# Weights through casting DMAs, q and k in longer runs, and a new order of loads, in a fused attention and SwiGLU kernel

## The chip, the cores and the metric

One core of one Trainium2 chip. The metric is device time in microseconds (us) of one execution. All executions in this study counted as fast (none stood apart by its time or its granted clock), so all numbers may be compared. The engines are PE (matmul), PEld (its weight load), DVE (VectorE), ACT (ScalarE), POOL (GpSimd) and SP (issues DMAs).

## The reference

Attention over q, k, v of shape (4, 8, 768, 64): a query sees its last 96 keys and the first 8 keys of its sequence ("global" keys), with a linear bias by distance. Then RMS norm and a SwiGLU feed-forward of 3072 tokens (512 to 1536 to 512). Inputs and output are fp32; both kernels multiply in bf16.

```python
scores = scale * np.matmul(q, k.transpose(0, 1, 3, 2))
keep = is_global | is_local                     # key < 8, or 0 <= query - key < 96
dist = np.where(is_global & ~is_local, 96., np.abs(rel))
a = softmax(np.where(keep, scores - slopes * dist, -1e9))
x = (a @ v).transpose(0, 2, 1, 3).reshape(3072, 512)
xn = x / np.sqrt(np.mean(x * x, -1) + 1e-6) * rms_g
g, val = xn @ w_gate, xn @ w_val
return (g * sigmoid(g) * val) @ w_out
```

## The kernel before

The tokens go through in 8 chunks of 384 (three blocks of 128; chunk c is half c % 2 of batch c // 2). A chunk has four head pairs. For a pair: POOL casts q and k to bf16 (`cast`), PE transposes them (`tr`), DVE copies the transposes out of PSUM into `qT` and `kT` (`cp`), PE makes two groups of scores (`qk`: d=0 against the query's own block, d=1 against the block before, whose first eight keys are overwritten with the global keys), ACT takes exponentials (`ex`), DVE masks, PE multiplies by v (`av`) and DVE normalises (`norm`). Then come the RMS norm (`ssq`, `rstd`, `xn`), a transpose (`xtr`) and its eviction by ACT (`xev`). The feed-forward has 12 F units a chunk (w_gate and w_val matmuls, tanh, two DVE multiplications) and O units (w_out).

The order is fixed by hand in slots: one unit per slot, with a `pre` list before its matmuls and a `post` list after. The program order that results is the order of each engine's queue, and also what decides which of two accesses of a buffer comes first.

Weights come in fp32 through a staging pool and are cast by three engines:

```python
def load_w(what, s):
    if what == "o":
        t = wstg.tile([128, 4, 512], F32, tag="ws", name="wso")
        nc.sync.dma_start(t, moe_w_out[ds(512 * s, 512)].rearrange("(f p) c -> p f c", p=128))
    ...
def cast_w(what, s):
    t = wst.pop((what, s))
    if what == "g":
        nc.vector.tensor_copy(w_gate[:, :, ds(512 * s, 512)], t)
    elif what == "v":
        nc.gpsimd.tensor_scalar(w_val[:, :, ds(512 * s, 512)], t, 0.5, None, op0=ALU.mult)
    else:
        nc.scalar.copy(w_out[:, ds(4 * s, 4), :], t)
```

q, k and v come per head pair, a token of a block per partition (runs of 256 bytes); the loads of chunk 0 are shared by SP and ACT. The copy of transposes and the global keys:

```python
def cp(c, p):                                   # DVE
    ...
    nc.vector.tensor_copy(qT, t[:, 0])
    nc.vector.tensor_copy(kT[:, ds(CH * half, CH)], t[:, 1])

def ex(c, p, d):                                # ACT
    ...
    if d == 0:                                  # global keys into the first 8 columns of each block
        nc.gpsimd.tensor_copy(
            kT.rearrange("p (j t) -> p j t", t=128)[:, lo:hi, 0:NG], _brd(kT[:, 0:NG], 1, hi - lo))

def attention(c, starts, gap, early=False):
    for p, a in enumerate(starts):
        at_slot(pre, a - 1, cast, c, p)
        at_slot(post, a, tr, c, p)
        at_slot(pre, a + 1, cp, c, p)
        at_slot(post, a + 1, qk, c, p, 0, early)
        at_slot(pre, a + 2, ex, c, p, 0)
        at_slot(pre, a + 3, mask, c, p, 0)
        at_slot(post, a + 1 + gap, qk, c, p, 1, early)
        ...
        at_slot(post, a + 3 + gap, av, c, p)
        at_slot(pre, a + 4 + gap, norm, c, p)
    ...
attention(0, [1, 3, 5, 7], 1, early=True)       # then F units of chunk 0, with attention 1 among them
```

The softmax here doesn't subtract the row's maximum and nothing guards it: scores larger than these inputs give would overflow.

## Time and profile before

| | before |
|---|---|
| median of 4 runs | 325.44 us (324.91 to 325.94) |
| span of the profiled run | 324.4 us, mean granted clock 0.967 |
| first scores / first gate matmul of chunk 0 / of chunk 1 | 17.4 / 45.5 / 92.0 us |
| two steady chunks | 65.0 us |

The gate matmuls are the `gps` group, the first of a chunk's feed-forward. Of chunk 1's, two ran at 92.0 us and the rest from 93.7; the prediction cuts at 93.7. The period of two steady chunks is the distance between the first gate matmuls of chunks two apart.

The prediction shows the stages and the timelines. Three more lines will be needed for comparison. The first two are PE's waits from 93.7 us to the end (who waited, for whom: us in all, times, longest); the third is from POOL's timeline of set-up (start, length).

```profile
PE trp L226 <- ACT xT L349: 5.7, 5, 1.1
PE avp L303 <- DVE P L288: 4.0, 12, 0.6
```

### The profile page before, as it was taken

The numbers are of one execution on the slowest core, as the hardware profiler recorded it, in microseconds if no ns is written. First come the engines' busy times: TensorE is split into PE (matmuls) and PEld (weight loads), VectorE is DVE, ScalarE is ACT, GpSimd is POOL, SyncE is SP. The second block draws the span as 40 slices with busy tenths as digits, with TensorE's granted clock in tenths as the row PEclk, the third lists the DMA queues.
The fourth block names the chain that finished last, engine by engine and source line by source line (L and its number), as shares of the span: only waits on it lengthen the run. The fifth ranks groups of instructions, "written<-read, shape, count | busy, mean of one in ns | idle before, by whom it ended". The sixth has DMA issues, their size and how long they took to land.

```text
span 324.4 us, 5608 instructions
## 1 busy us (share of the span) xinstructions
PE 258.3 (80%) x2033; PEld 147.0 (45%) x2048; DVE 210.1 (65%) x463; ACT 159.5 (49%) x334; POOL 110.4 (34%) x225
## 2 busy tenths in 40 slices
PE   1055065849379999899989998999899989999995
PEld 0033033525135555455446654654466546544652
DVE  7265747696717576389748963897489738962860
ACT  0445133524377365755465557564655575646331
POOL 6470879650325550101365501013655010001000
PEclk9999999786959999999999999999999999999999
DMA  9993096619992171897019007970100020002002
GB/s 174 264 261 129 0 246 190 230 33 315 218 217 59 61 155 32 181 239 116 2 65 179 3 2 179 239 117 2 66 32 3 2 81 16 2 2 97 0 3 97
DMA packets 83835, 34.96 MB, mean 108 GB/s; under 512 B 76128, under 2 KB 76128, under 8 KB 83808
## 3 DMA queue, kind: packets, MB, share of 16 engines
q1 hardware_dynamic: 79008, 33.43, 45.6%
q10 hardware_dynamic: 4800, 1.18, 2.1%
q8 instruction: 16, 0.26, 0.4%
q14 instruction: 11, 0.09, 0.1%
HBM read 28.31 MB, written 6.29 MB: 107 GB/s over the span
## 4 chain that ended last, share of the span: by engine, by line
PE 42%; DVE 30%; ACT 16%; issue 6%; DMA 2%; POOL 1%; ACTq 1%; DVEq 0%; POOLq 0%
PE ops L378 12%; PE gps L361 10%; PE vps L367 9%; DVE hb L371 7%; DVE u L370 7%; PE sc L255 4%; ACT P L266 4%; DVE xn L333 4%; ACT xT L349 4%; ACT t L364 3%; DVE P L285 3%; DVE P L288 3%; DVE w_gate L121 2%; ACT junk L319 2%; PE avp L303 2%
## 5 line engine op out<-in xcount | busy, mean ns | idle before, releaser
L266 ACT ACTIVATE P<-sc,bias 128x384 bf16<-128x384 f32 (+1 forms) x128 | 63.7, 551 | 49.7 <-PE sc L255 49.7
L361 PE MATMUL gps<-xT,w_gate 128*128 128x384 bf16 x384 | 83.8, 341 | 1.3 <-ACT xT L349 1.2
L367 PE MATMUL vps<-xT,w_val 128*128 128x384 bf16 x384 | 82.3, 339 | 0.0
L370 DVE SCALAR_TENSOR_TENSOR u<-t,gps 128x384 f32<-128x384 f32 x96 | 53.0, 552 | 28.8 <-ACT t L364 26.9
L364 ACT ACTIVATE t<-gps 128x384 f32<-128x384 f32 x96 | 47.2, 491 | 48.5 <-PE gps L361 48.3
L378 PE MATMUL ops<-w_out,hb 128*128 128x512 bf16 x273 | 66.6, 380 | 0.6
L371 DVE TENSOR_TENSOR hb<-u,vps 128x384 bf16<-128x384 f32 x96 | 53.2, 554 | 10.4 <-PE vps L367 0.8
L367 PEld LDWEIGHTS <-w_val 128*128 128x128 bf16 x384 | 39.0, 102 | 28.3 <-issue 5.3
L361 PEld LDWEIGHTS <-w_gate 128*128 128x128 bf16 x384 | 34.5, 101 | 24.5 <-issue 5.1
L274 POOL COPY kT<-kT 128x16 bf16<-128x16 bf16 x32 | 6.3, 197 | 112.1 <-PE sc L255 101.6
L255 PE MATMUL sc<-qT,kT 64*128 64x128 bf16 x352 | 22.9, 233 | 21.1 <-DVE kT L237 18.6
L378 PEld LDWEIGHTS <-hb 128*128 128x128 bf16 x288 | 26.4, 98 | 28.2
L333 DVE TENSOR_SCALAR xn<-xu,r 128x512 bf16<-128x512 bf16 x24 | 17.0, 762 | 17.7 <-POOL r L326 17.7
L349 ACT ACTIVATE xT<-xtp,rmsg 128x384 bf16<-128x384 bf16 x32 | 16.8, 578 | 22.2 <-PE xtp L341 22.2
L255 PEld LDWEIGHTS <-kT 64*128 64x128 bf16 x352 | 10.9, 97 | 35.1 <-DVE kT L237 21.2
L319 ACT ACTIVATE junk<-xu 128x512 bf16<-128x512 bf16 x24 | 14.8, 619 | 20.9 <-DVE xu L312 20.8
L341 PE MATMUL xtp<-ident,xn 128*128 128x128 bf16 x96 | 10.6, 240 | 18.1 <-DVE xn L333 15.5
L288 DVE TENSOR_TENSOR P<-P,md 128x512 bf16<-128x512 bf16 (+1 forms) x32 | 15.7, 490 | 13.1 <-ACT P L266 13.1
L324 POOL TENSOR_SCALAR m<-ssq 128x3 f32<-128x3 f32 x8 | 1.6, 197 | 65.0 <-ACT junk L319 65.0
L226 PE MATMUL trp<-ident,qb 128*128 128x128 bf16 x96 | 11.7, 237 | 11.6 <-ACT xT L349 6.8
L209 POOL CAST V<-sv 128x384 bf16<-128x384 f32 (+1 forms) x40 | 20.3, 532 | 1.0 <-DMA sv<-in_v_dram 1.0
L236 DVE COPY qT<-trp 128x384 bf16<-128x384 bf16 x32 | 11.5, 359 | 13.8 <-PE trp L226 13.8
(54 smaller groups left out, 287.9 us busy)
## 6 DMA issues: line engine op xcount, KB each, us to landing
out_dram<-osb SPq DMA_DIRECT2D x24, 256.0 KB, 2.0
sq<-in_q_dram SPq DMA_DIRECT2D x12, 384.0 KB, 5.7
sk<-in_k_dram SPq DMA_DIRECT2D x12, 384.0 KB, 6.3
sv<-in_v_dram SPq DMA_DIRECT2D x12, 384.0 KB, 6.4
wsg<-in_moe_w_gate_dram SPq DMA_DIRECT2D x3, 1024.0 KB, 5.4
wsv<-in_moe_w_val_dram SPq DMA_DIRECT2D x3, 1024.0 KB, 5.5
wso<-in_moe_w_out_dram SPq DMA_DIRECT2D x3, 1024.0 KB, 6.9
sq<-in_q_dram SPq DMA_DIRECT2D x16, 96.0 KB, 3.6
```

The lines of the kernel that those rows point to most:

```text
L255: nc.tensor.matmul(sc[hh][:, ts(i, 128)], kT[r, ts(J, 128)], qT[r, ts(i, 128)], start=True, stop=True)
L266: nc.scalar.activation(P[:, hh, lo:HB, :], sc[hh][:, ds(128 * lo, CH - 128 * lo)], AF.Exp, bias=(bias1 if d else bias0)[:, h:h + 1], scale ...
L288: nc.vector.tensor_tensor(P[:, :, lo:HB, :], P[:, :, lo:HB, :], _brd(md1[:, ds(2 * p, 2)], 2, HB - lo), op=ALU.mult)
L319: nc.scalar.activation(junk, xus[c][:, i].rearrange("p h d -> p (h d)"), AF.Square, accum_out=at["ssq", c][:, i:i + 1])
L333: nc.vector.tensor_scalar(t[:, i], xus[c][:, i].rearrange("p h d -> p (h d)"), r[:, i:i + 1], None, op0=ALU.mult)
L349: nc.scalar.activation(xTs[c][:, 2 * j + cc, :], t[:, cc], AF.Copy, scale=rmsg[:, 2 * j + cc:2 * j + cc + 1])
L361: nc.tensor.matmul(g[:, 0:CH], w_gate[:, cc, ts(f, 128)], xTs[c][:, cc, :], start=(cc == 0), stop=(cc == CC - 1))
L364: nc.scalar.activation(t, g[:, 0:CH], AF.Tanh, scale=0.5)
L367: nc.tensor.matmul(vv[:, 0:CH], w_val[:, cc, ts(f, 128)], xTs[c][:, cc, :], start=(cc == 0), stop=(cc == CC - 1))
L370: nc.vector.scalar_tensor_tensor(u, t, 1.0, g[:, 0:CH], op0=ALU.add, op1=ALU.mult)
L371: nc.vector.tensor_tensor(hb[c][:, f, :], u, vv[:, 0:CH], op=ALU.mult)
L378: nc.tensor.matmul(o, hb[c][:, f, ts(j, 128)], w_out[:, f, :], start=(f == 0), stop=(f == FC - 1))
```

## The change

The intent: no engine spends time on casting weights, ACT is free of DMA issues at the start, q and k come in fewer and longer pieces, and loads are asked for in the order in which they are needed.

```diff
     def load_w(what, s):                      # POOL issues; the DMA casts on its way
         if what == "o":
-            t = wstg.tile([128, 4, 512], F32, tag="ws", name="wso")
-            nc.sync.dma_start(t, moe_w_out[ds(512 * s, 512)].rearrange("(f p) c -> p f c", p=128))
+            nc.gpsimd.dma_start(w_out[:, ds(4 * s, 4), :],
+                                moe_w_out[ds(512 * s, 512)].rearrange("(f p) c -> p f c", p=128))
 ...                                           # cast_w is gone; its 0.5 moves to the output eviction
+            nc.sync.dma_start(                 # three neighbouring tokens per partition, 768 bytes
+                st[name, c][:, ds(h0, n)],
+                src[b, ds(h0, n), ds(CH * half, CH)].rearrange("h (p i) d -> p h (i d)", i=HB))
 ...                                           # v: one block, all heads, per DMA
+    nc.vector.tensor_tensor(gl1, _brd(slope[0:NG], 2, 128), _brd(iidx, 1, H), op=ALU.mult)
 ...                                           # set-up: two such in place of five small ones per head
+            if c == 0 and name == "q":
+                nc.scalar.copy(o, i)           # chunk 0: q cast by ACT, k by DVE
+            elif c == 0:
+                nc.vector.tensor_copy(o, i)
 ...
+    def glob_v(c):                             # global rows of v: a DMA issued by POOL
 ...
-        nc.vector.tensor_copy(qT, t[:, 0])
-        nc.vector.tensor_copy(kT[:, ds(CH * half, CH)], t[:, 1])
+        nc.vector.tensor_copy(qT.rearrange("p (t i) -> p t i", i=HB),
+                              t[:, 0].rearrange("p (i t) -> p t i", i=HB))
+        nc.vector.tensor_copy(kT[:, ds(CH * half, CH)].rearrange("p (t i) -> p t i", i=HB),
+                              t[:, 1].rearrange("p (i t) -> p t i", i=HB))
 ...
+        late = 2 if early else 0               # norm of chunk 0 two slots later
-            at_slot(pre, a + 4 + gap, norm, c, p)
+            at_slot(pre, a + 4 + gap + late, norm, c, p)
 ...                                           # xtr and xev two slots later after xn
-    n0 = attention(0, [1, 3, 5, 7], 1, early=True)
+    cast_v(0, i) for the blocks; glob_v(0)     # (written shorter here)
+    for s in range(2):
+        load_w("g", s)
+        load_w("v", s)
+    stage(1)
+    nc.gpsimd.memset(st["q", 1][0:1, 0, 0:1], 0.0)   # holds chunk 1's loads back till here
+    load_qk(1, 0, 4); load_qk(1, 4, 4); load_v(1, i) for the blocks
+    load_w("g", 2)
+    load_w("v", 2)
+    for s in range(3):
+        load_w("o", s)
+    n0 = attention(0, [1, 3, 5, 7], 0, early=True)
-    units += [None] * 4
+    units += [None] * 11
-    e1 = attention(1, [s0 - 1, s0 + 1, s0 + 3, s0 + 5], 2)
+    e1 = attention(1, [s0 + 5, s0 + 7, s0 + 9, s0 + 11], 1)
-        e = attention(c, [f - 23, f - 19, f - 15, f - 11], 2)
+        e = attention(c, [f - 25, f - 21, f - 17, f - 13], 2)
```

Since a partition now holds tokens 3t, 3t+1, 3t+2, the transposes come out interleaved, and the two DVE copies put them back in order by reading PSUM with a step.

## The prediction

> **What bounds it now.** I first cut the span into stages, at the moments when the matmuls of a stage begin, and asked for the busy time of each engine in each stage. Columns: start:end in us, length, then busy us and (instructions) of each engine, granted clock, DMA share, GB/s.
>
> ```profile
> 0.00:17.40 17.40, 0.98 (x8) 0.51 (x10) 9.41 (x54) 3.28 (x3) 8.88 (x30) 1.00 1.08 230
> 17.40:31.40 14.00, 8.53 (x98) 5.58 (x98) 8.82 (x22) 7.29 (x16) 6.97 (x20) 1.00 0.80 194
> 31.40:45.50 14.10, 2.59 (x19) 1.90 (x20) 7.77 (x5) 4.05 (x10) 11.81 (x16) 1.00 0.32 93
> 45.50:93.70 48.20, 31.30 (x227) 17.47 (x226) 31.74 (x53) 19.34 (x39) 24.48 (x36) 0.84 0.87 200
> 93.70:321.40 227.70, 214.94 (x1687) 121.56 (x1701) 152.39 (x330) 125.47 (x267) 58.27 (x124) 0.99 0.35 75
> ```
>
> The reader is to see three regions. Up to 17.4 us PE does almost nothing (set-up). From 17.4 to 93.7 us (attention of chunk 0, its normalisation, feed-forward of chunk 0 with attention of chunk 1) PE is busy 42.4 of 76.3 us. From 93.7 us on, PE is busy 94%: seven chunks at 227.7/7 = 32.5 us each. A change that touches no matmul can win only a little there, and up to some tens of us in the first 93.7.
>
> Then the timelines of single engines (start, length, engine, line, what; in brackets idle time and its releaser) for the waits of the first part:
>
> ```profile
> 10.36 1.28 ACT L168 ACT_TABLE_LOAD   x1 [10.36 <-DMA sv<-in_v_dram]
> 13.69 1.21 DVE L175 TENSOR_TENSOR gl<-gl,inv 8x1024 f32<-8x1024 f32 x1 [5.84 <-ACT gl L169]
> 17.37 0.34 PEld L255 LDWEIGHTS <-kT 64*128 64x128 bf16 x8 [11.89 <-DVE kT L237]
> ...
> 34.61 5.38 POOL L123 TENSOR_SCALAR w_val<-wsv 128x2048 bf16<-128x2048 f32 x1
> 34.66 6.49 DVE L333 TENSOR_SCALAR xn<-xu,r 128x512 bf16<-128x512 bf16 x3 [3.25 <-POOL r L326]
> ...
> 91.24 1.90 ACT L125 CAST w_out<-wso 128x2048 bf16<-128x2048 f32 x1
> 93.02 1.06 ACT L349 ACTIVATE xT<-xtp,rmsg 128x384 bf16<-128x384 bf16 x2
> ```
>
> ACT issues loads of k and v, and those waits sit in front of its table load and mask exponentials; DVE waits for them, and the first scores wait for DVE. Later the xn scaling takes 6.49 us beside a POOL weight cast, where in steady state three of them take 0.88 (at 130.84 us, POOL idle) to 2.4 us. Just before the feed-forward of chunk 1, an ACT weight cast of 1.9 us stands ahead of the last xT eviction.
>
> By line and form, the casts that the change removes:
>
> ```profile
> L123 POOL TENSOR_SCALAR w_val<-wsv 128x2048 bf16<-128x2048 f32 x3 | 16.1, 5369 | 0.0
> L121 DVE CAST w_gate<-wsg 128x2048 bf16<-128x2048 f32 x3 | 8.8, 2948 | 0.0
> L125 ACT CAST w_out<-wso 128x2048 bf16<-128x2048 f32 x3 | 5.7, 1892 | 0.0
> L236 DVE COPY qT<-trp 128x384 bf16<-128x384 bf16 x32 | 11.5, 359 | 13.8 <-PE trp L226 13.8
> L237 DVE COPY kT<-trp 128x384 bf16<-128x384 bf16 x32 | 11.1, 347 | 0.0
> ```
>
> The last two rows are not removed but become strided.
>
> **The Trainium skill.** "SBUF — State Buffer", section "Who interferes with whom": DVE copies, casts and tensor_scalar in two-port modes and any GpSimd instruction exclude each other for the whole instruction. The trace agrees: the same w_gate cast takes 1.36 us with no POOL weight cast beside it, 3.48 and 4.00 beside one. "DMA: Bandwidth & Descriptors", section "SWDGE vs HWDGE vs iDMA": a cast during DMA needs the software path, whose descriptors GpSimd cores write; its section "Anatomy of one DMA" puts about 2 us fixed on such a DMA, mostly completion, and calls generation "small, variable". The trace of before has no such DMA, so nothing there tells how long POOL is held. "VectorE: DVE Perf Modes", section "What auto-detection actually checks": the doubled 16-bit mode needs steps of one. The trace fits: bf16 copies from PSUM take 0.35 us for 384 elements, f32 work on 384 takes 0.55 (hb row, 554 ns).
>
> **The change, part by part.**
>
> (1) Set-up. ACT loses its 12 DMA issues, so the exponentials start when gl1 and gl0 exist. Twice 1.2 us on DVE (the form of L175) after iota gives about 4.3; the mask copy 0.4; ACT twice 1.05, to 6.8; DVE 1.2 + 1.2 for the m products, to 9.2; memsets, k cast, transposes, two copies: first scores near 12 instead of 17.4 us. Loads of 768-byte runs instead of 256 should not hold this up: 2.36 MB at the 230 GB/s of this stage is 10 us, and the first pair is there near 4.
>
> (2) A new gate on POOL. As built, POOL's order for chunk 0 is: three v casts, two VG copies, one software DMA for the global rows, four weight DMAs, a memset, five weight DMAs, and only then the four kT copies on which each pair's second score group (d=1) waits. Before, the first kT copy was at 17.97 us. The last two weight DMAs also wait for the global-row DMA and the first weight slice to land. My estimate: v casts and VG copies finish near 11 (loads in order, each 0.2 to 0.26 MB, about 1 us), the global-row DMA near 12, nine weight DMAs at about 1.1 us of POOL each (an estimate; no row of before measures it) gives 22, the landing of slice 0 near 17 not being last. So d=1 of pair 0 goes at 22 instead of 18.2, although its first scores could be 5 us earlier.
>
> (3) Attention of chunk 0. Before, first scores at 17.4 to the last avp at 30.5: 13 us. From the gate: first pair 2.1 us (exponential 0.84, mask 0.45, avp 0.5, waits), three more at 3.4 (one 0.5 of scores, 1.05 + 0.84 ACT, 0.45, 0.5), so 22 + 12.3 = 34.3. From last avp to first gate matmul: 14.9 us before, less 6.5 - 2.3 = 4.2 of the POOL-blocked xn: 10.7. First gate matmul at 45, against 45.5. Here the gain of set-up is spent on the gate.
>
> (4) Feed-forward 0 with attention 1, 48.2 us. Removed from its path: two w_gate casts on DVE, 3.5 + 4.0 = 7.5, and the 1.9 us on ACT. Added: strided qT/kT copies, 4 pairs x 2 x 0.2 = 1.6 on DVE. Cross-check from below: six units at 1.35 (PE) = 8, then DVE work 12 x 1.1 + 4 x (1.1 cp + 1.2 masks + 0.76 norm) = 25.4 of which 6.6 is done, so 18.8 more, then from the last norm 10.5 to the next gate matmul, and some 2 of chain losses: 39.5. Removing and adding gives 40.4. I take 39.5. The schedule starts attention 1 six slots later and leaves 11 empty slots instead of 4, so no more than this is won.
>
> (5) Steady chunks. PE work is the same. Attention sits two slots earlier, which takes its transposes away from the single transpose buffer just ahead of a feed-forward; before, six such waits on the xT eviction cost 6.8 us together; part comes back as a wait of the gate matmul. Gain about 0.4 each, 2 us in all. Against it 0.4 us DVE per pair where DVE is at 90% in parts. Span 93.7 to end was 230.7; I take 228.7.
>
> Sum: 45 + 39.5 + 228.7 = 313.2 of span, plus 1.15 (325.55 - 324.4): 314.4. As generation may be shorter than I set, and the change was presumably tuned with the first part in view, I lower it to 312.
>
> **Rivals.** First, generation is short (0.5 us each): then the gate falls at about 18.5, set by slice 0 landing, everything after it 3.5 earlier: 310, or 306 if stage (4) also sheds its chain losses. For it: the skill's "small, variable". Against: 512 runs per weight DMA. Second, generation is long (3 us each, or blocked by DVE): the gate falls at 39, first gate matmul at 62, and the gain of stage (4) only pays for it: 330. Against: while the gate holds, DVE has little to do, so it blocks little. Third, DVE becomes the bound in steady state: 1.6 us a chunk more on an engine 67% busy over the stage; if all of it were on the path, 7 x 1.6 = 11, time 323, within 2%. Against: PE is busy 9.74 of 10 us from 140 to 150 us, DVE 8.98. Fourth, weights arrive late: 9.4 MB plus 4.7 MB of chunks 0 and 1 at 230 GB/s are 61 us, but the slices are needed in order, the first near 45 and w_out after 85, so hidden.
>
> **Range and chances.** The gate time carries most: 18.5 to 30 moves the result by -3.5 to +8; stage (4) by 4 either way; steady state by 3 either way. So 312, 303 to 322. Faster by over 2% means under 319.0: 0.80. Within 2%: 0.16. Slower: 0.04.
>
> **What would show it.** First scores near 12 us and a PE idle time after them, ended by the POOL kT copy, show (1) and (2). POOL rows of weight DMA issues show their length. xn of chunk 0 at 1 to 2.5 us shows (3); the distance from first gate matmul to that of chunk 1 near 39.5 shows (4); qT and kT copies at 0.55 us and a steady chunk of 32.2 to 32.5 us show (5). The prediction is wrong if POOL is held much longer or shorter than 10 us by the weight DMAs, or if the steady chunk moves by over 1 us.

## More of the kernel before

```profile
2.06 0.29 POOL L158 TENSOR_SCALAR_AFFINE_SELECT md<-md 128x128 bf16<-128x128 bf16 x1
```

In the steady part PE has only two waits of note: transposes behind the eviction of xT, which uses the one transpose buffer, and the second avp group behind a mask. No wait for `kT` is among them.

## The result, and the profile after

| | before | after |
|---|---|---|
| median of 4 runs | 325.44 us | 317.62 us (316.90 to 318.47) |
| profiled span, clock | 324.4, 0.967 | 316.8, 0.973 |
| first scores | 17.4 | 13.1 |
| first gate matmul, chunk 0 | 45.5 | 39.5 |
| first gate matmul, chunk 1 | 92.0 | 81.8 |
| from there to the end of the span | 232.4 | 235.0 |
| two steady chunks | 65.0 | 66.6 |

The ratio of after to before is 0.9761 (95% interval 0.9730 to 0.9792): faster by 2.4%. A ratio here is the mean time of one kernel's fast runs over that of the other's of the same rounds, so it isn't quite the ratio of the medians quoted.

The stages of the kernel after, with the columns of the prediction's first fence (busy us and instructions of PE, PEld, DVE, ACT, POOL, then clock, DMA share, GB/s). The first cut at chunk 1 was set at 81.98, which is 0.2 us behind its first gate matmul (81.78); the texts go by the matmul.

```profile
0.00:13.13 13.13, 1.00 (x6) 0.48 (x7) 9.49 (x27) 4.10 (x5) 7.96 (x20) 1.00 0.69 180
13.13:31.40 18.27, 7.82 (x97) 5.67 (x98) 9.51 (x23) 7.92 (x18) 8.45 (x16) 1.00 0.99 180
31.40:39.53 8.13, 2.02 (x17) 1.35 (x15) 2.11 (x5) 3.00 (x8) 2.06 (x4) 1.00 1.19 221
39.53:81.98 42.45, 28.53 (x237) 16.67 (x236) 25.41 (x51) 19.05 (x40) 12.88 (x26) 0.84 0.74 161
81.98:316.80 234.82, 214.51 (x1685) 119.94 (x1696) 161.80 (x330) 123.05 (x264) 51.38 (x112) 0.99 0.25 69
```

Set-up is 4.3 us shorter, the attention of chunk 0 is 4.3 us longer (18.3 against 14.0), the way from there to the feed-forward is 6 us shorter (8.1 against 14.1), and the stage of both chunks is 4 us shorter (42.3 against 46.5, both to the first of chunk 1's gate matmuls). The cut at 31.4 is the same moment in both, and not quite the same point of the work: the last avp ended at 30.6 before and at 31.7 after. The weight casts, 31 us on three engines before (the first three rows of the prediction's last fence), are gone. The last row is the surprise: the long part, which the change was to shorten a little, is longer, and DVE has 161.8 us to do in it.

From the timelines of PE, POOL, ACT and DVE:

```profile
13.13 0.71 PE L261 MATMUL sc<-qT,kT 64*128 64x128 bf16 x10 [1.12 <-DVE kT L242]
2.23 1.12 POOL L164 TENSOR_SCALAR_AFFINE_SELECT md<-md 128x128 bf16<-128x128 bf16 x1
...
13.49 0.78 POOL L223 DMA_DIRECT2D VG<-V  x1 [0.32 <-POOL VG L218]
14.28 0.82 POOL L122 DMA_DIRECT2D w_gate<-in_moe_w_gate_dram  x1
...
18.90 2.29 POOL L118 DMA_DIRECT2D w_out<-in_moe_w_out_dram  x3
21.17 0.34 POOL L280 COPY kT<-kT 128x16 bf16<-128x16 bf16 x2
0.80 1.28 ACT L174 ACT_TABLE_LOAD   x1 [0.80 <-PEq L509]
35.78 1.35 DVE L339 TENSOR_SCALAR xn<-xu,r 128x512 bf16<-128x512 bf16 x3 [3.28 <-POOL r L332]
```

ACT loads its table at once, as intended. POOL's queue is held from 13.5 to 21.2 us by ten DMA issues; only then do the copies of the global keys run. And yet the first row has ten score matmuls in one go at 13.13: six of d=0 and four of d=1. The d=1 matmuls of pair 0 did not wait for the copy at 21.17.

**They did not wait because they come first in the program.** With `gap` 0, `qk(c, p, 1)` stands in slot a+1, while the copy is written in `ex(c, p, 0)` in slot a+2. The order is well defined, so there is no race, but the second score group of block 2 in chunk 0 (tokens 256 to 383 of batch 0) is made against keys 128 to 135 where the global keys should be. I recomputed the reference in floating point with this error put in: the output of these rows moves by at most 0.0070 (rms 0.0013), where the output has rms 1.41 and a largest value of 8.7. The comparison with the reference doesn't see it: with these inputs the scores are small, and the exponentials stay near what the bias alone gives. The kernel after is wrong in this place.

DVE's copies, by line and form (busy us, mean ns of one | idle before, releaser), and PE's waits in the whole run and in the last stage:

```profile
L240 DVE COPY qT<-trp 128x384 bf16<-128x384 bf16 x32 | 17.7, 552 | 7.2 <-PE trp L230 6.9
```

```profile
PE sc L261 <- DVE kT L242: 12.7, 22, 2.4
...
PE avp L305 <- DVE xu L318: 9.1, 3, 3.3
```

```profile
PE sc L261 <- DVE kT L242: 6.9, 16, 0.5
PE avp L309 <- DVE P L294: 4.5, 12, 0.6
PE gps L367 <- ACT xT L355: 2.2, 7, 0.3
```

Read against the lines of before: the qT copy takes 552 ns where it took 359; in the last stage the wait of transposes for the xT eviction (5.7 us) is gone; but scores now wait 6.9 us for kT, and gate matmuls 2.2 us for the xT eviction (1.2 before). And in chunk 0, avp waits three times 3 us for the normalisation of the pair before, since there is one avp buffer and `late` puts that normalisation two slots back.

### The profile page after: what moved, and what is told of

The parts are those of the page before. It is cut to its first block, busy times and chain, and to the rows that moved or that the text cites. A ratio compares the mean times of both kernels' runs of the same rounds, so it can differ in the third digit from the quotient of the medians.

```text
span 316.8 us, 5462 instructions
## 1 busy us (share of the span) xinstructions
PE 253.9 (80%) x2034; PEld 144.1 (45%) x2048; DVE 208.3 (66%) x435; ACT 157.1 (50%) x335; POOL 82.7 (26%) x177
## 2 busy tenths in 40 slices
DMA packets 50747, 30.38 MB, mean 96 GB/s; under 512 B 26592, under 2 KB 47584, under 8 KB 50720
## 4 chain that ended last, share of the span: by engine, by line
PE 39%; DVE 21%; ACT 10%; issue 5%; POOL 2%; DVEq 0%; POOLq 0%; ACTq 0%
PE ops L384 16%; PE vps L373 7%; PE gps L367 7%; DVE hb L377 6%; DVE u L376 5%; PE sc L261 4%; ACT P L272 3%; ACT xT L355 3%; ACT t L370 3%; DVE P L294 2%; DVE kT L242 2%; DVE qT L240 2%; ACT junk L325 2%; PE xtp L347 2%; DVE xu L318 1%
## 5 line engine op out<-in xcount | busy, mean ns | idle before, releaser
L367 PE MATMUL gps<-xT,w_gate 128*128 128x384 bf16 x384 | 82.9, 334 | 3.0 <-ACT xT L355 2.2
L373 PE MATMUL vps<-xT,w_val 128*128 128x384 bf16 x384 | 79.8, 331 | 0.0
L373 PEld LDWEIGHTS <-w_val 128*128 128x128 bf16 x384 | 38.1, 99 | 28.2 <-issue 4.5
L384 PEld LDWEIGHTS <-hb 128*128 128x128 bf16 x288 | 26.2, 98 | 28.4
L261 PE MATMUL sc<-qT,kT 64*128 64x128 bf16 x352 | 22.2, 232 | 13.7 <-DVE kT L242 12.7
L305 PE MATMUL avp<-V,P 128*128 128x65 bf16 x192 | 18.5, 201 | 10.1 <-DVE xu L318 9.1
L261 PEld LDWEIGHTS <-kT 64*128 64x128 bf16 x352 | 11.1, 99 | 29.6 <-DVE kT L242 18.3
L240 DVE COPY qT<-trp 128x384 bf16<-128x384 bf16 x32 | 17.7, 552 | 7.2 <-PE trp L230 6.9
L389 ACT ACTIVATE osb<-ops 128x512 f32<-128x512 f32 x24 | 14.3, 597 | 14.8 <-PE ops L384 14.8
L339 DVE TENSOR_SCALAR xn<-xu,r 128x512 bf16<-128x512 bf16 x24 | 11.7, 540 | 14.7 <-POOL r L332 14.7
L305 PEld LDWEIGHTS <-P 128*128 128x128 bf16 x192 | 14.3, 102 | 13.7 <-DVE xu L318 9.9
L216 POOL CAST V<-sv 128x512 bf16<-128x512 f32 x24 | 15.3, 645 | 15.0 <-DMA sv<-in_v_dram 15.0
## 6 DMA issues: line engine op xcount, KB each, us to landing
w_gate<-in_moe_w_gate_dram POOLq DMA_DIRECT2D x3, 512.0 KB, 11.1
w_val<-in_moe_w_val_dram POOLq DMA_DIRECT2D x3, 512.0 KB, 14.3
w_out<-in_moe_w_out_dram POOLq DMA_DIRECT2D x3, 512.0 KB, 26.5
```

The costliest lines, as they stand in the source:

```text
L240: nc.vector.tensor_copy(qT.rearrange("p (t i) -> p t i", i=HB), t[:, 0].rearrange("p (i t) -> p t i", i=HB))
L261: nc.tensor.matmul(sc[hh][:, ts(i, 128)], kT[r, ts(J, 128)], qT[r, ts(i, 128)], start=True, stop=True)
L305: nc.tensor.matmul(o[:, i, hh, :], P0[:, hh, i, :], V1[b % 2][:, I, h, :], start=True, stop=(I == 0))
L367: nc.tensor.matmul(g[:, 0:CH], w_gate[:, cc, ts(f, 128)], xTs[c][:, cc, :], start=(cc == 0), stop=(cc == CC - 1))
L373: nc.tensor.matmul(vv[:, 0:CH], w_val[:, cc, ts(f, 128)], xTs[c][:, cc, :], start=(cc == 0), stop=(cc == CC - 1))
L384: nc.tensor.matmul(o, hb[c][:, f, ts(j, 128)], w_out[:, f, :], start=(f == 0), stop=(f == FC - 1))
```

## The experiments

Theories at this point. **A:** the strided copies lengthen the steady part, since scores wait for them; the first part owes its gain to the casts and to set-up, less what the late normalisation and the crowd of loads take back. **B, the rival:** the copies lie beside other work, and it is the moved slots that lengthen the steady part; chunk 0 isn't bound by the normalisation, and weights alone would do it. In the texts A is the theory and B the rival of each run. Twelve kernels ran, three rounds each beside the kernel before, whose medians were 326.09, 326.08 and 326.21 us. The change itself wasn't run again, and before's medians are 0.6 to 0.8 us higher than beside the change (325.44), so a difference from the change of under about 1 us says nothing.

### What the strided copies cost: flat_copies

```diff
-        nc.vector.tensor_copy(qT.rearrange("p (t i) -> p t i", i=HB), t[:, 0].rearrange(...))
-        nc.vector.tensor_copy(kT[...].rearrange("p (t i) -> p t i", i=HB), t[:, 1].rearrange(...))
+        nc.vector.tensor_copy(qT, t[:, 0])
+        nc.vector.tensor_copy(kT[:, ds(CH * half, CH)], t[:, 1])
```

Wrong: tokens stay interleaved.

> The changed kernel with the qT and kT copies out of PSUM made contiguous again, everything else left (the tokens of q and k then stand in the wrong order, so the result is wrong on purpose; no instruction is added or removed). Theory A (the strided copies, 0.55 instead of 0.35 us, are what made the steady chunks 0.85 us slower, through the scores' wait for kT): copies back at 0.35 us, two steady chunks 64.9 us or less instead of 66.6, total 311 to 314. Rival B (the attention placed two slots earlier and the V copies spread over every chunk made them slower): two chunks stay at 66.2 or more, total 316.5 or more.

Measured: 311.18 us (ratio 0.9547, 0.9521 to 0.9574), period 64.7 us. Its copies, and the two longest of PE's waits from the first gate matmul of chunk 1 to the end:

```profile
L240 DVE COPY qT<-trp 128x384 bf16<-128x384 bf16 x32 | 11.3, 353 | 8.1 <-PE trp L230 7.8
```

```profile
PE avp L307 <- DVE P L292: 4.6, 12, 0.6
PE gps L365 <- ACT xT L353: 2.2, 7, 0.3
```

The wait for DVE's kT is gone, and 6.4 us with it. The 64 copies got shorter by 0.20 us each, 12.7 us in all: half of that was on the path. Per chunk, 1.6 us of added DVE work (8 copies by 0.2) lengthened the period by 1.0 (1.9 per two chunks). A holds.

### The same with the tokens in the right order: blocks_later

```diff
+            if c < 2: ...                      # as in the change
+            for i in range(HB):                # later chunks: block by block, runs of 256 bytes
+                nc.sync.dma_start(
+                    st[name, c][:, ds(h0, n), ds(D * i, D)],
+                    src[b, ds(h0, n), ds(CH * half + 128 * i, 128)].rearrange("h p d -> p h d"))
 ...
+        if c >= 2:                             # and contiguous copies there
+            nc.vector.tensor_copy(qT, t[:, 0])
+            nc.vector.tensor_copy(kT[:, ds(CH * half, CH)], t[:, 1])
```

> The changed kernel with q and k of chunks 2 to 7 loaded in blocks of 128 tokens (three DMAs of 256-byte runs in place of one of 768-byte runs), so that their copies out of PSUM are contiguous; the result is right. Theory A (the copies are the cost, the longer runs save nothing once loads are hidden): two steady chunks 64 to 65 us instead of 66.6, total 312.5 to 314. Rival B (the long runs were worth it): waits for the loads appear in the steady chunks, total 316.5 or more.

Measured: 311.95 us (0.9567, 0.9548 to 0.9586), period 64.7 us. Nearly all of the gain is there with the tokens in the right order (chunk 0's too early read of the global keys is still in it, as in every kernel made from the change but keys_first, keys_dve, best and best2): the 256-byte runs, in place of 768, cost nothing where the loads are asked for long ahead. The longer runs bought nothing in the steady part.

### The slots: old_slots

```diff
-        e = attention(c, [f - 25, f - 21, f - 17, f - 13], 2)
+        e = attention(c, [f - 23, f - 19, f - 15, f - 11], 2, lag=3)   # xtr at e + 3 again
```

> The changed kernel with the attention of chunks 2 to 7 in the slots of before (two later) and the transposes of xn at the old distance. Theory A (strided copies are the cause): no change or slightly slower, 317 to 319, two steady chunks 66.5 to 67. Rival B (the slots are the cause): two steady chunks near 65, total 313 to 315.

Measured: 317.42 us (0.9733, 0.9714 to 0.9753), period 66.4 against 66.6. B falls: the slots are not the cause. Its waits of PE from 79.2 us to the end:

```profile
PE trp L230 <- ACT xT L355: 5.7, 5, 1.1
PE sc L261 <- DVE kT L242: 5.0, 12, 0.5
...
PE gps L367 <- ACT xT L355: 0.3, 1, 0.3
```

So it was the new slots that took the transposes' wait away, but nothing was won by it: scores wait 1.9 us more for kT in the new slots, gate matmuls 1.9 us more for xT, and the period is no shorter.

The run teaches something on stage tables, too. Its first gate matmul of chunk 1 came 2.6 us earlier than in the change (39.3 to 79.2 us), and what followed was 1.7 us longer (236.7). Attention of chunk 2 that begins two slots later simply falls behind the mark: PE has 231 instructions in the stage in place of 237. So the last two stages should be read as a sum: 277.3 us in the change, 276.6 here.

### The gate that the prediction expected: keys_first

```diff
-    n0 = attention(0, [1, 3, 5, 7], 0, early=True)
+    n0 = attention(0, [1, 3, 5, 7], 1, early=True)
```

> The changed kernel with one slot more between the two score groups in chunk 0, so that the copy of the global keys into kT, which GpSimd makes, comes ahead of the scores that should read it (in the changed kernel it comes after them). Theory A (the gate of the prediction exists once that order is kept): first d=1 scores wait for GpSimd until about 21.3 us instead of starting at 13.7, first gate matmul at 42 to 45 us, total 320 to 323. Rival B (GpSimd is no gate): PE's wait for the GpSimd copy is below 1 us, total 317 to 319.

Measured: 322.11 us (0.9878, 0.9851 to 0.9904), first gate matmul of chunk 0 at 43.6. From PE's timeline:

```profile
12.86 0.61 PE L261 MATMUL sc<-qT,kT 64*128 64x128 bf16 x8 [1.12 <-DVE kT L242]
21.08 0.29 PE L261 MATMUL sc<-qT,kT 64*128 64x128 bf16 x2 [7.61 <-POOL kT L280]
```

In the right order the gate is there: 7.6 us of waiting for POOL, up to 21.08. In this version the change gains 1.2% in place of 2.4: as long as POOL makes the copy, half of the gain comes from reading the global keys too early.

### The right order without the gate: keys_dve

```diff
-            nc.gpsimd.tensor_copy(
+            (nc.vector if c == 0 else nc.gpsimd).tensor_copy(
                 kT.rearrange("p (j t) -> p j t", t=128)[:, lo:hi, 0:NG], _brd(kT[:, 0:NG], 1, hi - lo))
 ...
+    n0 = attention(0, [1, 3, 5, 7], 1, early=True)
```

> The changed kernel in the right order of chunk 0's key copy, as in the run of 322.1 us, but with that copy made by VectorE. Theory A (the 4.5 us were GpSimd's queue, held by the weight DMAs, and not the extra slot): PE's wait of 7.6 us is gone, first gate matmul at 38.5 to 40.5 instead of 43.6, total 316.5 to 318.5. Rival B (the order itself costs): 320 or more.

Measured: 317.29 us (0.9733, 0.9695 to 0.9771), first gate matmul of chunk 0 at 37.5. The copy takes 0.17 to 0.30 us on DVE, and PE waits 0.2 us for it, once. So the 4.8 us that keys_first lost were the queue of POOL and not the copy, and a correct version costs nothing.

### The late normalisation: norm_early

```diff
-        late = 2 if early else 0
+        late = 0
```

> The changed kernel with the normalisation of chunk 0's pairs put back to two slots earlier. Theory A (PE's three waits of 3 us for xu in chunk 0, 9.1 us in all, come from the single avp buffer together with the late normalisation): the waits shrink to 1 us or less each, the first gate matmul comes at 35 to 37 instead of 39.5 us, total 313.5 to 315.5. Rival B (the chain of exponentials and masks of each pair takes the same time whatever the place of the normalisation): first gate matmul at 38.5 or later, total 317 or more.

Measured: 319.09 us (0.9786, 0.9765 to 0.9807). The first gate matmul of chunk 0 came at 35.6, 3.9 us earlier, as A has it; the total did not follow, so A's total was a miss. In POOL's timeline, the casts of chunk 1's first two blocks of v:

```profile
45.27 0.62 POOL L216 CAST V<-sv 128x512 bf16<-128x512 f32 x1 [12.47 <-DMA sv<-in_v_dram]
49.92 0.62 POOL L216 CAST V<-sv 128x512 bf16<-128x512 f32 x1 [3.34 <-DMA sv<-in_v_dram]
```

Chunk 1's v lands at 45 and at 50 us, much as in the change (casts at 46.0 and 50.2, where chunk 0 ended 3.9 us later), and POOL waits for it, and with it all that stands behind in POOL's queue, the q and k casts of chunk 1's later pairs included. The gain turned into a longer wait for a load. (Up to 1.8 of the 4.8 us by which the stage of both chunks grew may be something else: the granted clock in it was 0.81 against 0.84 in the change, and PE was busy 30.1 us in place of 28.3.)

### Why v lands late: norm_early_wout_late, and wout_late

```diff
     load_w("g", 2)
     load_w("v", 2)
-    for s in range(3):
-        load_w("o", s)
 ...
+    for s in range(3):
+        at_slot(pre, s0 + 12 + s, load_w, "o", s)     # asked for just after chunk 0's F units
```

The first of the two has `late = 0` as well, the second only this.

> The changed kernel with the earlier normalisation of chunk 0 (which alone gave 319.1 us although its first gate matmul came at 35.6 instead of 39.5) and with the three w_out slices asked for only after the feed-forward of chunk 0. Theory A (in that run the gain turned into a wait for chunk 1's v, which lands after 45 us because all nine weight slices stand ahead of or beside it): chunk 1's v lands before 41 us, the wait of GpSimd for it shrinks, first gate matmul of chunk 1 at 77 to 79.5 instead of 82 to 84, total 312.5 to 315. Rival B (v is held by something else, the queue's own waits): v still lands after 44 us, total 317 or more.

Measured: 313.90 us (0.9624, 0.9606 to 0.9642). First gate matmuls at 35.3 and 77.7. The first cast of chunk 1's v, in the same view:

```profile
40.05 0.62 POOL L216 CAST V<-sv 128x512 bf16<-128x512 f32 x1 [7.55 <-DMA sv<-in_v_dram]
```

With 1.5 MB of w_out (as written, in bf16) out of the way, v is there 5 us earlier, and the normalisation's 3.9 us reach the end: 3.7 us less than the change.

> The changed kernel with only the three w_out slices asked for later. With the early normalisation this was worth 5 us (319.1 to 313.9). Theory A (in the changed kernel chunk 1's v, landing at 46 and 50 us, already holds the attention of chunk 1, so its landing earlier helps here too): chunk 1's first gate matmul at 79.5 to 81 instead of 82, total 315 to 316.5. Rival B (there v was just off the path): 317 to 318.

Measured: 318.47 us (0.9763, 0.9723 to 0.9802): no gain, a miss for A and the result that B expects. v landed earlier here also (the cast at 40.2 us, against 46.0 in the change), but with the late normalisation it wasn't what chunk 1 waited for. Two limits side by side, of which the later one counts: taking away either one alone gains nothing, both together 3.7 us.

### The weights alone: weights_only, weights_gated

Both are the kernel before with casting weight DMAs and nothing else of the change. In weights_only they are asked for where the staged loads were; in weights_gated they stand later in the program. The cut shows where weights_gated puts them.

```diff
-    load_w("g", 0)
-    load_w("v", 0)
     for p in range(2):
         load(0, 1, p, (nc.sync,) * 3)
-    load_w("g", 1)
+    for s in range(3):
+        at_slot(pre, 7 + s, load_w, "g", s)
+        at_slot(pre, 7 + s, load_w, "v", s)
+        at_slot(pre, s0 + 3 + s, load_w, "o", s)
```

> The kernel before with one part of the change alone: the nine weight slices come by casting DMAs from GpSimd's queue at the places in the program where they were loaded, and the nine casts are gone (the factor 0.5 goes into the output eviction). Loads of q, k, v, their layout, the slots and the set-up are those of before. Theory A (the casts were what stages 3 and 4 lost): xn of chunk 0 at 1 to 2.5 us instead of 6.5, first gate matmul at 40.5 to 42.5 instead of 45.5, first gate matmul of chunk 1 at 80 to 84 instead of 93.7, steady chunks as before at 32.4, total 312 to 315.5, so better than the whole change. Rival B (the weight DMAs hold GpSimd ahead of the casts of q, k and v, or weights compete with these loads, and what the casts cost comes back as such waits): total 317 or more.

Measured: 320.91 us (0.9843, 0.9826 to 0.9859), a miss for A and within what B said (317 or more). The stage from first gate matmul to that of chunk 1 fell from 46.5 to 36.4 us, as A has it:

```profile
50.50:86.90 36.40, 26.15 (x225) 15.38 (x223) 23.82 (x51) 16.88 (x36) 11.04 (x30) 0.93 0.77 136
```

Not all of this need be the casts. The granted clock is 0.93 in this stage, where it was 0.85 before (from 45.5 to 92.0 us), and PE is busy 26.2 us in place of 30.4 with nearly the same matmuls. So up to about 4 of the 10 us may be the clock; no run separates the two.

And first scores came at 26.2 us in place of 17.4. The timelines of POOL and ACT (ACTq is ACT's issuing of DMAs):

```profile
3.27 0.97 POOL L111 DMA_DIRECT2D w_gate<-in_moe_w_gate_dram  x1
...
15.93 3.25 ACTq L97 DMA_DIRECT2D sk<-in_k_dram  x2
19.20 1.28 ACT L155 ACT_TABLE_LOAD   x1 [19.20 <-DMA sk<-in_k_dram]
```

Weights asked for at 3.3 us run beside chunk 0's loads; ACT's issues stretch to 19.2 us (10.4 before), and table and mask exponentials stand behind them.

> The kernel before with the casting weight DMAs alone, as in the run where they were asked for at the old places (320.9 us), but the gate and value slices asked for only when GpSimd has cast all of chunk 0 (slots 7 to 9), and w_out during the feed-forward of chunk 0. Theory A (in that run the first two slices, asked for at once, came ahead of chunk 0's loads and moved the first scores from 17.4 to 26.2 us, while the stage from first to next first gate matmul had fallen from 48.2 to some 37): first scores back at 17 to 18, first gate matmul at 40.5 to 43, chunk 1's at 77 to 81, total 309 to 313. Rival B (asked for later, the weights land too late for the feed-forward of chunk 0): waits of the gate matmuls or of chunk 1's loads, total 315 or more.

Measured: 314.10 us (0.9619, 0.9578 to 0.9659), just above what A expects. First scores are back at 17.4, first gate matmuls at 43.5 and 80.1. The issues still sit in POOL's queue ahead of one kT copy:

```profile
31.33 0.29 PE L242 MATMUL sc<-qT,kT 64*128 64x128 bf16 x2 [2.79 <-POOL kT L261]
```

This one part, with its gate, is 3.5 us faster than the whole change: without the strided copies, without the new set-up, and with the global keys right. In this the rival was right: weights alone do more than the whole change did.

### The parts together: best, best2

best is the change with keys_dve, `late = 0`, w_out asked for later and blocks_later.

> A version from what was found: the changed kernel with the global keys copied in chunk 0 by VectorE, and one slot more so that the copy comes ahead of its readers; normalisation of chunk 0 early; w_out late; q and k of chunks 2 to 7 in blocks of 128. If the parts add up: first gate matmul at 36 to 38 us, that of chunk 1 at 78 to 80, two steady chunks 64 to 65, total 308 to 311. If GpSimd's queue or the loads of chunk 1 take the gain back: 312 to 316.

Measured: 307.11 us (0.9419, 0.9392 to 0.9447), 5.8% under the kernel before and 10.5 us under the change, with the global keys in the right order. The three parts had gained 0.3, 3.7 and 5.7 us alone, 9.7 together (0.3 being within the noise), so they add up, with 10.5 measured.

best2 takes away the memset that holds chunk 1's loads back, starts attention 1 four slots earlier and leaves 7 empty slots in place of 11.

```diff
-    nc.gpsimd.memset(st["q", 1][0:1, 0, 0:1], 0.0)
-    units += [None] * 11
+    units += [None] * 7
-    e1 = attention(1, [s0 + 5, s0 + 7, s0 + 9, s0 + 11], 1)
+    e1 = attention(1, [s0 + 1, s0 + 3, s0 + 5, s0 + 7], 1)
```

> The combined version of 307.1 us with chunk 1's loads asked for at once behind those of chunk 0 instead of after four weight DMAs, and the attention of chunk 1 four slots earlier, with four empty slots less. If the late attention of chunk 1 is what keeps the stage from first to next first gate matmul at 41.5 us, where the weights alone had some 37: stage at 37 to 39, total 302.5 to 305. If loads or VectorE take it back: 306 to 309.

Measured: 306.84 us (0.9404, 0.9372 to 0.9437): the same as best, a miss for the first expectation and what the second says. The stage of both chunks fell from 41.3 to 39.2 us, but chunk 0 gave it back: its first gate matmul came at 36.6 in place of 34.6. In PE's timeline:

```profile
18.91 0.22 PE L320 MATMUL avp<-VG,P 128*128 128x65 bf16 x1 [1.73 <-DMA VG<-V]
```

The 16 KB DMA of global v rows now runs beside chunk 1's loads and lands later, which is 1.7 of the 2.0 us. The earlier loads take back what the earlier attention may gain; the two weren't run apart.

| kernel | median us | ratio to before | gate matmul chunk 0 | chunk 1 | period |
|---|---|---|---|---|---|
| the change | 317.62 | 0.9761 | 39.5 | 81.8 | 66.6 |
| flat_copies (wrong) | 311.18 | 0.9547 | 38.0 | 80.2 | 64.7 |
| blocks_later | 311.95 | 0.9567 | 39.2 | 81.0 | 64.7 |
| old_slots | 317.42 | 0.9733 | 39.3 | 79.2 | 66.4 |
| keys_first | 322.11 | 0.9878 | 43.6 | 84.9 | 66.7 |
| keys_dve | 317.29 | 0.9733 | 37.5 | 81.0 | 66.7 |
| norm_early | 319.09 | 0.9786 | 35.6 | 82.7 | 66.7 |
| norm_early_wout_late | 313.90 | 0.9624 | 35.3 | 77.7 | 66.7 |
| wout_late | 318.47 | 0.9763 | 39.2 | 81.2 | 66.7 |
| weights_only | 320.91 | 0.9843 | 50.5 | 86.9 | 65.1 |
| weights_gated | 314.10 | 0.9619 | 43.5 | 80.1 | 65.1 |
| best | 307.11 | 0.9419 | 34.6 | 75.9 | 64.7 |
| best2 | 306.84 | 0.9404 | 36.6 | 75.8 | 64.7 |

## Why the prediction was right, point by point

The time (312 predicted, 317.6 measured) is inside the range and the class is right. But that the sum came so near is in part luck, by errors that offset: 45 + 39.5 + 228.7 = 313.2 was predicted, and 39.5 + 42.3 + 235.0 = 316.8 measured, so -5.5, +2.8 and +6.3. The last step, from 314.4 down to 312 on a guess about generation and tuning, went the wrong way. A steady chunk went from 32.5 to 33.3 us: outside the 32.2 to 32.5 named as the sign of (5), inside the 1 us named as the sign of being wrong.

**(1) Set-up: right.** First scores at 13.1 (12 predicted, 17.4 before). The last 1.1 us were missed because DVE and POOL were taken to be independent there. Two affine_selects on POOL took 1.12 and 1.16 us in place of 0.29 and 0.37, while DVE made gl1 and gl0, and DVE then waited 0.7 us for POOL; the two multiplications of the m products took 1.67 and 1.51 us in place of 1.2 each, while POOL cast v. No run takes this apart, so it is argued from the times that overlap.

**(2) The gate on POOL: its end was right, the wait was not there.** POOL's queue held the kT copies until 21.17 (22 predicted), again by two errors that offset: the issues began at 13.5 in place of 12, and the nine weight DMAs took 0.76 to 0.85 us each in place of 1.1, an estimate that no row stood behind. The failed step is "the four kT copies on which each pair's second score group (d=1) waits": I knew the order on POOL, but did not read that `gap` 0 puts the reader ahead of the writer in the program. keys_first, with the right order, has the gate at 21.08 and its first gate matmul at 43.6, near the 45 predicted, though by parts that offset: 14.7 us from the gate to the end of the last avp (12.3 predicted) and 7.9 from there (10.7).

**(3) Attention of chunk 0: two errors.** Without the gate, the first gate matmul came at 39.5 and not 45. From the last avp to it took 7.9 us (10.7 predicted), with the three xn at 1.35 us, within the 1 to 2.5 predicted. (Some 1.9 of the 2.8 us of difference are again a matter of the mark: before, chunk 1's first transposes and their wait stood ahead of the gate matmul.) Against that stands a wait that I did not foresee: 9.1 us of PE behind the late normalisation. norm_early shows what it costs the first part, 3.9 us. norm_early_wout_late and wout_late show that on this path it stood beside the landing of v, and the later of the two counted.

**(4) Both chunks: 42.3 against 39.5, most of it a matter of the mark.** By old_slots, whose stage is 39.9 us, 2.4 of the 2.8 us are bookkeeping: attention of chunk 2 that now stands ahead of the mark. (The cross-check, added up again, gives 39.3 and not 39.5.) Whether the 9.4 us of casts went as reckoned is not shown: weights alone, at the old places, bring this stage from 46.5 to 36.4, but at a higher granted clock, as said there. In best2 attention 1 is earlier, with fewer empty slots and earlier loads, and the stage is 2.1 us shorter, so the 11 empty slots may cost what I had only noted as a limit; undoing them gained nothing in the end.

**(5) Steady chunks: the sign was wrong.** I set 2 us of gain from the slots against copies that I took as hidden, and said 228.7 where 235.0 was measured. The failed step is "Against it 0.4 us DVE per pair where DVE is at 90% in parts", which was named and then given no number. The size of the copy was right (0.55 us), and so was the third rival's mechanism, which allowed up to 11 us if all were on the path: flat_copies measures 6.4 for all chunks, about half. The reason is in the waits: scores follow the copy at once, so a longer copy shows as PE waiting for kT. The gain of the slots didn't come: the transposes' wait went, as I said, but came back as others, and old_slots shows no loss from undoing them (66.4 against 66.6). Without strided copies the period is 64.7 against 65.0 before, but these two kernels differ in more than the slots.

**Rivals.** The first (short generation, a gate at 18.5) and the second (long, at 39) are both out: 0.8 us per issue, and POOL free at 21.2. The third is in (5). The fourth asked whether weights arrive late; they did not, but w_out, asked for early, delayed chunk 1's v, a loser that I had not thought of.

**What stays open.** The sum of the last two stages is 277.3 us, where 268.2 was predicted: 9.1 over. flat_copies, from whose profile the same sum is 271.5, takes off 5.8. The other 3.3 are not settled run by run; best has 270.3 for it, and best2, with attention 1 earlier as well, 268.9, so the placement of chunk 1's work is a likely part of it, but these two change several things at once. The granted clock in the stage of both chunks (0.81 to 0.94 over the runs) is another part that no run isolates.

## What to carry to other kernels

A load layout with longer runs (50,747 DMA packets in the whole run here, in place of 83,835) has to be undone by some engine if it interleaves the tokens: price that copy, and see in the waits whether something follows it at once, for then a good part of its added time (here half) is on the path even where its engine seems to have room. A DMA issue is an instruction in its engine's queue: look at what stands behind it (here 7.6 us of gate, removed by moving a copy of 0.2 to 0.3 us to another engine), and ask for loads in the order of need. Where two limits end at nearly the same time, removing only one shows nothing, so test them together as well. When a wait that you expect is absent from the trace, check the program order of writer and reader before you count it as a gain; a comparison of outputs may not see the difference.

## What the Trainium skill lacked or had wrong

- "DMA: Bandwidth & Descriptors", section "Anatomy of one DMA — SWDGE (gpsimd) path", calls descriptor generation "small, variable" and gives no time for which GpSimd's own queue is held by one DMA; elsewhere the page has only a latency to the first byte. The runs show 0.74 to 0.85 us for a casting DMA of 512 KB (0.97 for the first one in weights_only and in weights_gated) and 0.67 to 0.78 for the 16 KB DMAs of global rows: nearly fixed, and in front of everything behind it on that queue (7.61 us of gate in keys_first). The section's fit for one DMA by itself says nothing on nine in a row: w_gate, w_val and w_out took 11.1, 14.3 and 26.5 us (medians) from issue to landing.
- The same page, section "Queues, rings and completion order", says that an engine switches between queue rows packet by packet, but not what a load on one row loses to casting loads on another. Here chunk 1's v was cast at 45.3 us with w_out queued early and at 40.1 with w_out asked for later (norm_early, norm_early_wout_late). That the loss is shared in the way that the section describes was not tested.

No run showed the cited sections to be wrong. The about 2 us that "Anatomy of one DMA" puts on one such DMA fit the 16 KB DMAs of global rows, which landed 2.2 us (median) after their issue in the kernel after. The condition in "VectorE: DVE Perf Modes", section "What auto-detection actually checks" (16-bit, steps of one), agrees with the runs: reading 384 bf16 elements a partition from PSUM with a step takes 552 ns, without one 353.
